# A transformer block on one Trainium2 core: roots by Newton steps on VectorE, first queries feature by feature, weights in 20 pieces, zero products by streamed share, single exponentials

## The chip, the cores and the metric

The kernel runs on one core of a Trainium2 chip. A core has five engines that run side by side, each through its own instruction queue in order: TensorE (PE in the profile; its weight loads are PEld), VectorE (DVE), ScalarE (ACT), GpSimd (POOL) and SyncE (SP), which here only issues DMAs. Sixteen DMA engines move data between the device's memory and the on-chip SBUF. TensorE writes its results to PSUM, eight banks of 128 partitions by 512 float32.

The metric is the device time of one execution in microseconds, the median of several runs.

## The reference

One pre-norm block over 2048 tokens of width 640, in bfloat16: attention with 32 query heads of 20 features that share one key and one value head, then a gated GELU layer with 1536 hidden features.

```python
def _layernorm(x, axis=-1, eps=1e-5):
    m = jnp.mean(x, axis=axis, keepdims=True)
    v = jnp.var(x, axis=axis, keepdims=True)
    return (x - m) / jnp.sqrt(v + eps)

def _A_ref(x, wq, wk, wv, wo):            # H = 32, Dh = 20
    q = (x @ wq).reshape(B, S, H, Dh) ... # heads first
    k = x @ wk                            # one head for all queries
    v = x @ wv
    scores = einsum("bhqd,bkd->bhqk", q, k) * Dh ** -0.5
    o = einsum("bhqk,bkd->bhqd", softmax(scores), v)
    return o ... .reshape(B, S, H * Dh) @ wo

def _B_ref(x, w_gate, w_up, w_down):
    return (gelu(x @ w_gate) * (x @ w_up)) @ w_down

h  = x + _A_ref(_layernorm(x), wq, wk, wv, wo)
h2 = h + _B_ref(_layernorm(h), w_gate, w_up, w_down)
```

There is no mask: 32 heads x 2048 queries x 2048 keys make 134 million exponentials.

## The kernel before, in words

**Tiling.** The tokens are 16 tiles of 128 rows. A *pack* is the work on four score tiles at once: eight matmuls of 20 features by 256 queries (L1009) fill four PSUM banks of 128 keys x 512. There are 512 packs, so 2048 score tiles. Each tile is exponentiated by one of two engines: ScalarE with its table (L1400, into `pa`), one tile per instruction or two that lie in neighbouring banks, or VectorE by arithmetic on the bits of the number (L1462, into `pd`), to which GpSimd adds two shifted copies by 64-bit integer adds (L1545). The sums over the keys (L1073, 128 x 32 by 256 columns) collect in an accumulator bank, with a column of ones for the denominator. Eight packs in a row make a *unit*; when a unit's products are all in, its accumulator is copied (L1108 or L1109 into `osb`), turned by a DMA transpose (`onu<-osb`, L681), divided by its denominator on VectorE (L720, L715 into `onq`), turned again (`onT<-onq`, L734) and multiplied by `wo`.

**LayerNorm.** For x (first) and for h (second): statistics on VectorE (L427, L434, L431), the root, a normalized copy `xn_tmp` (L541 on ScalarE or L543 on VectorE), and a DMA transpose `xn1T<-xn_tmp` (L525) that SyncE issues. The root of the first five groups of x tiles is a power on GpSimd (L464), which loads a library of instructions for it; a second library for the integer adds is loaded after the last of them (L460), and VectorE takes no score tile before that. All other groups take three Newton steps on VectorE (L471 to L492).

**Queries.** `xn1T` times `wq` gives queries token by token in PSUM; a copy to `qtok` (L642, L643) and a DMA transpose `qT<-qtok` (L655) bring the features onto partitions, where the packs need them.

**What sets the order.** A planner in the kernel file simulates five queues while the program is built: at each moment the engine that is free first takes the best task that its table of costs says is ready. The result is a fixed order of instructions on each engine, with semaphore waits between them; nothing is decided on the chip. The table `PRM` holds the planner's limits. `act_tile` takes one or two tiles, two only if at least `pair_min` are ready. `pe_decide` chooses between packs, sums over keys, pieces of projections (`issue_piece`) and *zero products*: matmuls of a zero tile into a free bank (L1280), issued where nothing else fits and TensorE was busy for less than `z_use` of the last 3400 ns by the planner's own times (`pe_use`).

**DMAs.** SyncE issues nearly all of them, in one queue. x tiles come first, then `wk`, `wv`, `wq` in two halves; the four large weights (`wo`, `wg`, `wu`, `wd`, one DMA each, L905) follow after 30 us of planned time. When the last score tile is done the rest of the gated layer for the last tokens runs alone (L560).

## Time and profile before

| | |
|---|---|
| median of 3 runs | 799.32 us (797.0 to 800.6) |
| profiled execution | 798.73 us, span of the trace 796.9 us |
| granted TensorE clock, mean | 0.949 |
| busy PE / DVE / ACT / POOL | 750.0 / 678.5 / 688.9 / 570.7 us |
| score tiles on ScalarE / VectorE | 1269 (939 alone, 165 pairs) / 779 |
| first and last start of a ScalarE exponential | 22.2 us, 750.4 us |
| HBM read / written | 12.18 / 2.62 MB |

The profile is one execution. An engine is busy when one of its instructions runs; waiting, branching and issuing DMAs do not count. In the page's second part the span is cut into 40 slices of 20 us and each digit is the busy share in tenths. "PEclk" is the clock granted to TensorE, 1.00 being full speed; it was either 1.00 or 0.50, so that an average between them is a share of time. In tables of stages each engine has its busy time and, in brackets, how many of its instructions ran there. In rows of waits "A <- B" means that A's engine stood still until B's instruction was done. In groups of instructions, "busy, mean ns" is the time covered by any of them, and the mean length of one; instructions of an engine overlap, so that one costs less than its length.

### The profile page before, as it was taken

To read this page: it belongs to the slowest core of one execution; us is meant where nothing else is said; L and a number is where in the kernel's file an instruction comes from. 1 tells how busy PE (TensorE), PEld (TensorE's weight loads), DVE (VectorE), ACT (ScalarE), POOL (GpSimd) and SP (SyncE) were. 2 spreads that over 40 slices of the span, in tenths; PEclk is the share of its full clock that TensorE was granted. 3 is DMA by queue.
4 is the path that set the end of the run, shared out by engine and by line. 5 is a ranking of instruction groups with operands and counts; after the bars stand their busy time and mean duration, and the time that the engine had idled before them with its cause. 6 is when DMAs were issued, how large, how long until landed. Compare 5 with 4: busy or idle time off the path is not lost.

```text
span 796.9 us, 37265 instructions
## 1 busy us (share of the span) xinstructions
PE 750.0 (94%) x16170; PEld 406.0 (51%) x16170; DVE 678.5 (85%) x1432; ACT 688.9 (86%) x1217; POOL 570.7 (72%) x1396
## 2 busy tenths in 40 slices
PE   7886999989998999999999999999999999999998
PEld 5343445444454545445554554444554545455687
DVE  6936899988989899999899887998899989989653
ACT  2685899987899899999999997999999999989822
POOL 1325899888888788588888786577888877588600
PEclk8688899978899899999999998999999999999999
DMA  7796101010021103010012302020022101101110
GB/s 200 117 245 200 30 9 32 9 25 9 10 40 22 20 11 53 10 26 10 22 31 60 53 13 41 9 27 9 10 43 52 38 10 26 26 11 25 50 28 18
DMA packets 79602, 33.44 MB, mean 42 GB/s; under 512 B 69072, under 2 KB 78160, under 8 KB 79440
## 3 DMA queue, kind: packets, MB, share of 16 engines
q1 hardware_dynamic: 79296, 30.90, 18.7%
q8 instruction: 128, 2.10, 1.1%
q14 instruction: 34, 0.28, 0.1%
q10 hardware_dynamic: 144, 0.16, 0.1%
HBM read 12.18 MB, written 2.62 MB: 19 GB/s over the span
## 4 chain that ended last, share of the span: by engine, by line
PE 52%; DVE 28%; ACT 11%; DMA 6%; issue 2%; SPq 1%; POOL 0%; DVEq 0%
DVE pd L1462 20%; PE ps L1073 18%; PE ps L1009 15%; PE ps L563 12%; ACT pa L1400 10%; PE ps L560 6%; DMA onu<-osb 2%; DMA onT<-onq 1%; DVE onq L715 1%; PE ps L1280 1%; DMA xn1T<-xn_tmp 1%; DVE stats L434 1%; DMA qT<-qtok 1%; DVE osb L1109 1%; DVE xh L757 1%
## 5 line engine op out<-in xcount | busy, mean ns | idle before, releaser
L1400 ACT ACTIVATE pa<-ps 128x512 bf16<-128x512 f32 (+1 forms) x1104 | 634.0, 715 | 51.6 <-PE ps L1009 43.8
L1545 POOL INT64_ADD pd<-pd x1378 | 566.1, 432 | 156.6 <-DVE pd L1462 133.1
L1462 DVE TENSOR_SCALAR pd<-ps 128x512 uint16<-128x512 f32 x779 | 497.8, 681 | 57.9 <-PE ps L1009 55.0
L1009 PE MATMUL ps<-qT,kT 20*128 20x256 bf16 x4096 | 263.8, 281 | 29.5 <-DVE pd L1462 13.1
L1073 PE MATMUL ps<-pd,v_ext 128*32 128x256 bf16 x4674 | 265.6, 286 | 0.6 <-DVE pd L1462 0.2
L1073 PE MATMUL ps<-pa,v_ext 128*32 128x256 bf16 x2538 | 227.3, 286 | 1.9 <-issue 0.8
L1073 PEld LDWEIGHTS ps<-pd,v_ext 128*32 128x32 bf16 x4674 | 168.7, 99 | 50.7 <-issue 28.6
L1009 PEld LDWEIGHTS ps<-qT,kT 20*128 20x128 bf16 x4096 | 88.5, 93 | 199.2 <-DVE pd L1462 96.9
L1073 PEld LDWEIGHTS ps<-pa,v_ext 128*32 128x32 bf16 x2538 | 127.2, 99 | 28.8 <-issue 18.9
L563 PE MATMUL ps<-wd_sb,gbuf 128*32 128x320 bf16 x1104 | 53.0, 302 | 0.3 <-DVE pd L1462 0.2
L563 PE MATMUL ps<-xn1T,wg_sb 128*32 128x512 bf16 x720 | 50.2, 382 | 0.1
L563 PE MATMUL ps<-xn1T,wu_sb 128*32 128x512 bf16 x720 | 49.0, 381 | 0.2
L862 DVE TENSOR_TENSOR gbuf<-ps,gbuf 128x512 bf16<-128x512 f32 (+2 forms) x72 | 36.5, 508 | 8.6 <-ACT gbuf L831 6.1
L831 ACT ACTIVATE gbuf<-ps 128x128 bf16<-128x128 f32 (+1 forms) x36 | 11.3, 313 | 27.0 <-PE ps L560 27.0
L563 PEld LDWEIGHTS ps<-wd_sb,gbuf 128*32 128x32 bf16 x1104 | 23.4, 95 | 18.8 <-issue 12.2
L563 PE MATMUL ps<-wo_sb,onT 128*32 128x320 bf16 x600 | 27.7, 301 | 1.7 <-DMA onT<-onq 1.5
L1280 PE MATMUL ps<-zero 128*32 128x256 bf16 x460 | 23.0, 334 | 4.1 <-POOL halfc L376 1.0
L563 PEld LDWEIGHTS ps<-xn1T,wu_sb 128*32 128x32 bf16 x720 | 16.4, 96 | 18.0 <-issue 6.3
L715 DVE TENSOR_TENSOR onq<-onu,rcp 128x160 bf16<-128x160 bf16 (+1 forms) x56 | 24.8, 470 | 0.2
L882 DVE TENSOR_TENSOR xh<-xh,ps 128x320 bf16<-128x320 bf16 x32 | 15.3, 479 | 11.1 <-PE ps L560 11.1
L1109 DVE CAST osb<-ps 128x256 bf16<-128x256 f32 x47 | 19.5, 414 | 6.0 <-PE ps L1073 5.9
L563 PEld LDWEIGHTS ps<-xn1T,wg_sb 128*32 128x32 bf16 x720 | 15.4, 95 | 16.9 <-issue 7.8
(65 smaller groups left out, 379.8 us busy)
## 6 DMA issues: line engine op xcount, KB each, us to landing
out_dram<-xh SPq DMA_DIRECT2D x16, 160.0 KB, 1.8
xh<-in_A_x_dram SPq DMA_DIRECT2D x7, 320.0 KB, 4.2
xh<-in_A_x_dram SPq DMA_DIRECT2D x13, 160.0 KB, 3.0
wg_sb<-in_B_w_gate_dram SPq DMA_DIRECT2D x1, 1920.0 KB, 9.3
wu_sb<-in_B_w_up_dram SPq DMA_DIRECT2D x1, 1920.0 KB, 11.1
wd_sb<-in_B_w_down_dram SPq DMA_DIRECT2D x1, 1920.0 KB, 16.0
wq_sb<-in_A_wq_dram SPq DMA_DIRECT2D x2, 400.0 KB, 5.8
wo_sb<-in_A_wo_dram SPq DMA_DIRECT2D x1, 800.0 KB, 5.2
```

The costliest lines, as they stand in the source:

```text
L560: return e.matmul(o(b), l(None), r, start=st, stop=sp)
L563: ins = e.matmul(o(b)[32 * q:32 * q + 32], l(q), r, start=st, stop=sp, tile_position=(0, 32 * q))
L715: dve((lambda o, vi, ri: lambda e: e.tensor_tensor(o, vi, ri.unsqueeze(3).to_broadcast([P, vi.shape[1], 4, Dh]), ALU.mult))(o, vi, ri), c_ ...
L862: dve(lambda e: e.tensor_tensor(o, bank(bk, n), o, ALU.mult), c_dve(n), [("b", bk)] + gkeys(b, fc), gkeys(b, fc), 0.8, fin)
L882: dve(lambda e: e.tensor_tensor(xh[:, t % NXH, h * HALF:(h + 1) * HALF], xh[:, t % NXH, h * HALF:(h + 1) * HALF], bank(bk, HALF), ALU.add) ...
L1009: ins = e.matmul(ps[:, b * 512 + h * 256:b * 512 + h * 256 + 256], kT4[32 * r:32 * r + Dh, kt * P:(kt + 1) * P], qv[32 * r:32 * r + Dh], s ...
L1073: ins = e.matmul(ps[32 * r:32 * r + 32, ab * 512:ab * 512 + 256], v_ext[:, it["kt"], it["w"], :], it["ap"], start=st, stop=(j in ends), ti ...
L1109: return e.tensor_copy(o, i)
L1280: ins = e.matmul(ps[32 * q:32 * q + 32, b * 512:b * 512 + 256], zero[:, 0:32], zero[:], start=True, stop=True, tile_position=(0, 32 * q))
L1400: op = plan.commit("act", lambda e: e.activation(dst, src, ACT.Exp, scale=SM_SCALE), cost, L_ACT, [("b", b0 + i) for i in range(n)], [("pa ...
L1462: op = plan.commit("dve", lambda e: e.tensor_scalar(pd[:, 0, s * 512:(s + 1) * 512], bank(b), CH_A, CH_B, ALU.mult, ALU.add), c_dve(512), ...
L1545: op = plan.commit("pool", (lambda w, a, sh: lambda e: e.int64_add(pd64[:, w, a], pd64[:, 0, a], sh))(w, a, sh), k * 128 * 1.7 + 180.0, L_ ...
```

## The change

1. **Roots.** The power on GpSimd is gone. All 18 groups of tiles take the same chain of ten small VectorE instructions (seed from the bits in 16 bits, two Newton steps, a reciprocal). The first LayerNorm's groups are now [0], [1], and seven pairs. Tile 0 is normalized on VectorE straight from mean and root. The only library of GpSimd is loaded at the start (L394); at the program's end four small GpSimd instructions with two more library loads are added.
2. **First queries.** The queries of tile 0 for heads 0 to 15 are computed feature by feature (`wq` stationary, `xn1T` streamed, 80 matmuls of 128 columns) and copied to `qT` without a transpose. `wq` comes in 340 + 300 columns.
3. **Weights.** `wo` in 2 pieces, `wg`, `wu`, `wd` in 6 each, spaced by 3.5 us of planned time; each use waits for its piece alone. The second part of `wq` and x tiles 6 to 9 are issued later (5.5, 8 and 9.5 us of planned time).
4. **Zero products.** `pe_use` counts the time that streaming the columns takes at full clock, not planned busy time, over 3413 ns; the limit is 0.53 (0.6 in the head), and below 0.48 zero products are issued where nothing else is ready, even if the next pack might have to wait for them. They may also be added to an open accumulator. 228 + 232 of them become 276 + 392.
5. **Single exponentials.** `pair_min` 9 cannot be reached with eight banks: all 1267 of ScalarE's tiles are single.
6. Other limits of the planner move (`w_tol`, `slack`, `press_a`, `press_d`, `q_ahead`, `flex_d`, `age`, `res_d`, `m_head`), and with them much of the order.

```diff
@@ PRM
-    "w_tol": 1300.0,
+    "w_tol": 600.0,
-    "slack": 60.0,
+    "slack": 20.0,
-    "press_a": 3,
-    "press_d": 3,
+    "press_a": 5,
+    "press_d": 2,
-    "q_ahead": 2,
+    "q_ahead": 4,
-    "flex_d": 400.0,
-    "pair_min": 4,
-    "age": 1500.0,
+    "flex_d": 800.0,
+    "pair_min": 9,
+    "age": 1000.0,
-    "ln1g": [[0], [1], [2, 3], [4, 5], [6, 7], [8, 9, 10, 11], [12, 13, 14, 15]],
+    "ln1g": [[0], [1], [2, 3], [4, 5], [6, 7], [8, 9], [10, 11], [12, 13], [14, 15]],
-    "z_use": 0.6,
+    "z_use": 0.53,
+    "w_t0": 30000.0,
+    "w_dt": 3500.0,
+    "z_head": 0.6,
+    "z_fk": 2,
+    "z_force": 0.48,
...
+    pool(lambda e: e.int64_add(lib[:, 1, :].bitcast(mybir.dt.int64), lib[:, 0, :].bitcast(mybir.dt.int64), 0),
+         7000, ["lib0"], ["lib1"])
...
+    def pe_use(t):
+        u = 0.0
+        for a, z, st in reversed(pe_log):
+            if z < t - 3413.0:
+                break
+            u += st * (z - max(a, t - 3413.0)) / (z - a)
+        return u / 3413.0
...
+        steps = [
+            (lambda e: e.tensor_copy(vb, mv[:, ln, sl, 1]), [("mv", ln, t) for t in tiles], [K("vb")]),
+            (lambda e: e.tensor_scalar_add(veb, vb, EPS), [K("vb")], [K("veb")]),
+            (lambda e: e.tensor_scalar(y0.bitcast(U16), veb.bitcast(U16), -0.5, 24352.0, ALU.mult, ALU.add),
+             [K("veb")], [K("y0")]),
...
+            (lambda e: e.scalar_tensor_tensor(den, tt, 1.5, p, ALU.add, ALU.mult), [K("t"), K("p")], [K("den")]),
+            (lambda e: e.reciprocal(ln_r[:, ln, sl], den), [K("den")], [K("lr")]),
+        ]
...
-            task(("pool",), lambda e: e.tensor_tensor(ln_denb[:, ln, sl], ln_veb[:, ln, sl], halfc[:, 0:n], ALU.pow),
-                 700, L_POOL, [("veb", kk), "halfc"], [("den", kk)], prio - 1.0, pdone)
...
+    def q0_job(h):
+        g0 = 0 if h == "a" else 2
...
+                pieces.append((mm((lambda i: lambda b: ps[:, b * 512 + i * P:b * 512 + i * P + P])(i),
+                                  (lambda i, c: lambda q: wq_sb[:, c * D + 80 * (g0 + i) + 20 * q:
+                                                                c * D + 80 * (g0 + i) + 20 * q + 32])(i, c),
+                                  xn1T[:, c, 0:P], c == 0, c == NC_D - 1, False), c_mm(P) + 20.0,
+                               [("xn1T", 0), ("wq", 0)]))
...
-    for nm, o, v in (("wo", wo_sb, A_wo), ("wg", wg_sb, B_w_gate), ("wu", wu_sb, B_w_up), ("wd", wd_sb, B_w_down)):
-        sp_tasks.append(_Task(("sp",), (lambda o, v: lambda e: e.dma_start(o[:], cview(v)))(o, v), 1500, 12000,
-                              [], [nm], 9.0, None, lambda: plan.free["sp"] > 30000.0))
...
+    for i, (o, v, ks) in enumerate(pieces_w):
+        sp_tasks.append(_Task(("sp",), (lambda o, v: lambda e: e.dma_start(o, v))(o, v), 480, 3500,
+                              [], ks, 9.0 + 0.01 * i, None,
+                              (lambda i: lambda: plan.free["sp"] > PRM["w_t0"] + i * PRM["w_dt"])(i)))
...
+        if state["qk_left"] > 0 and not head and pe_use(t) < PRM["z_force"] and not (nr or piece is not None or opening is not None):
+            if zeros(PRM["z_fk"]):
+                return True
```

On **SyncE**, where the large weights are issued (the last x tiles' transposes, then weights, then the first finished unit), before:

```order
L525 DMA_TRANSPOSE xn1T<-xn_tmp 128x5x128 x4
L655 DMA_TRANSPOSE qT<-qtok 128x4x128
L905 DMA wo_sb<-in_A_wo_dram 128x5x640
L905 DMA wg_sb<-in_B_w_gate_dram 128x5x1536
L914 DMA xh<-in_A_x_dram 128x640 x3
L655 DMA_TRANSPOSE qT<-qtok 128x4x128
L914 DMA xh<-in_A_x_dram 128x640 x3
L905 DMA wu_sb<-in_B_w_up_dram 128x5x1536
L905 DMA wd_sb<-in_B_w_down_dram 128x12x640
L681 DMA_TRANSPOSE onu<-osb 128x4x128 x2
```

and now:

```order
L537 DMA_TRANSPOSE xn1T<-xn_tmp 128x5x128 x10
L669 DMA_TRANSPOSE qT<-qtok 128x4x128 x2
L955 DMA wo_sb<-in_A_wo_dram 128x2x640
L955 DMA wo_sb<-in_A_wo_dram 128x3x640
L669 DMA_TRANSPOSE qT<-qtok 128x4x128
L537 DMA_TRANSPOSE xn1T<-xn_tmp 128x5x128 x2
L955 DMA wg_sb<-in_B_w_gate_dram 128x5x256 x2
L971 DMA xh<-in_A_x_dram 128x640 x6
L669 DMA_TRANSPOSE qT<-qtok 128x4x128
L955 DMA wg_sb<-in_B_w_gate_dram 128x5x256 x3
L717 DMA_TRANSPOSE onu<-osb 128x4x128
```

A finished unit's transpose stands behind pieces, no longer behind whole weights. Up to the last of the sixteen `xn1T` there are now four `qT` and both pieces of `wo` in the queue, where there were six `qT`.

On **TensorE**, where one accumulator is finished and the next has too few products to open, so that packs (`ps<-qT,kT`) follow one another with hardly a sum over keys (`v_ext`) between them; before, around packs 107 to 110:

```order
L1009 MATMUL ps<-qT,kT 128x256 x8
L1073 MATMUL ps<-pd,v_ext 32x256 x4
L1009 MATMUL ps<-qT,kT 128x256 x16
L1280 MATMUL ps<-zero 32x256 x8
L1009 MATMUL ps<-qT,kT 128x256 x8
L1280 MATMUL ps<-zero 32x256 x12
```

and now, around packs 99 to 102:

```order
L1066 MATMUL ps<-qT,kT 128x256 x8
L1130 MATMUL ps<-pd,v_ext 32x256
L1066 MATMUL ps<-qT,kT 128x256 x8
L1270 MATMUL ps<-zero 32x256 x12
L1066 MATMUL ps<-qT,kT 128x256 x8
L1270 MATMUL ps<-zero 32x256 x24
L1066 MATMUL ps<-qT,kT 128x256 x8
L1270 MATMUL ps<-zero 32x256 x8
```

This place has 44 zero products now, the one before had 20.

On **VectorE** at the start, from the variance of tile 0 on (`ln_vb`), before:

```order
L449 CAST ln_vb<-mv 128x1
L431 BN_AGGR mv<-stats 128x2
L453 TENSOR_SCALAR ln_veb<-ln_vb 128x1
L449 CAST ln_vb<-mv 128x1
L434 BN_STATS stats<-xh 128x6
L453 TENSOR_SCALAR ln_veb<-ln_vb 128x1
```

and now:

```order
L488 CAST ln_vb<-mv 128x1
L463 BN_STATS stats<-xh 128x6
L489 TENSOR_SCALAR ln_veb<-ln_vb 128x1
L460 BN_AGGR mv<-stats 128x2
L463 BN_STATS stats<-xh 128x6
L490 TENSOR_SCALAR ln_y<-ln_veb 128x1
```

Each BN_STATS shown belongs to tile 2 or 3, whose load it needs. Now the chain of tile 0 stands behind it; the copy `xn_tmp` of tile 0 comes 28 instructions later than the first BN_STATS shown, and four of these are statistics.

More of the change, by code (lines that the diff above doesn't have):

```diff
@@ L491, in nden @@
-        def nden(op):
-            dve(lambda e: e.tensor_tensor(ln_denb[:, ln, sl], va, ya, ALU.mult), 65, [("nv", kk), ("ny", kk)],
-                [("den", kk)], prio - 1.0, c4)
-        def c4(op):
-            dve(lambda e: e.reciprocal(ln_r[:, ln, sl], ln_denb[:, ln, sl]), 75, [("den", kk)], [("lr", kk)],
-                prio - 1.0, c5)
+                chain(steps, c5)(None)
         def c5(op):
-            if ln == 0:
+            if ln == 0 and tiles[0] not in DIRECT:
                 dve(lambda e: e.scalar_tensor_tensor(ln_nb[:, sl], mv[:, ln, sl, 0], -1.0, ln_r[:, ln, sl], ALU.mult,
@@ L959, in dve_ok @@
     def dve_ok():
[L960 removed]
+        return pd_free[pd_next[0]]
     def est_banks(t):
@@ L1027, in issue_qk @@
             last = i == len(parts) - 1
[L1028 to L1029 removed]
+            op = pe(mk(part), (219.0 if last else 115.0) + sw, 53.3 * len(part), t_reads,
+                    [("b", b) for r, b in part], t, L_PE + (0.0 if last else 104.0))
             for r, b in part:
@@ L1201, in pe_decide, with zeros, zfn @@
                 piece = None
+        def zeros(k):
+            fb = [b for b in free_now if plan.ready("pe", ["zero"], [("b", b)]) <= t]
+            ac = [u["acc"] for u in accu if all(u["started"])]
+            if not (fb or ac):
+                return False
+            b = fb[-1] if fb else ac[0]
+            fresh = bool(fb)
+            def zfn(e):
+                ins = None
+                for q in list(range(4)) * k:
+                    ins = e.matmul(ps[32 * q:32 * q + 32, b * 512:b * 512 + 256], zero[:, 0:32], zero[:],
+                                   start=fresh, stop=fresh, tile_position=(0, 32 * q))
+                return ins
+            state["z"] = 1
+            sw = 0.0 if state["mode"] == "v" else SW
+            state["mode"] = "v"
+            pe(zfn, 110.0 * k + sw, 106.7 * k, ["zero"], [("b", b)], t)
+            return True
+        if state["qk_left"] > 0 and not head and pe_use(t) < PRM["z_force"] and not (nr or piece is not None or opening is not None):
+            if zeros(PRM["z_fk"]):
+                return True
         wready = nr >= 1 or opening is not None or piece is not None
@@ L1270, in pe_decide @@
             return do_pv()
[L1271 to L1294 removed]
+        if (state["qk_left"] > 0 or PRM["z_tail"]) and fits(110.0 + swv - slack) and pe_use(t) < (PRM["z_head"] if head else PRM["z_use"]):
+            return zeros(1)
+        return False
     def next_piece(t, may, pick_bank):
@@ L1503, in dve_decide @@
                 opts.append((pr, len(opts), tk))
+            elif tk.prio < 0.0 and state["kv_left"] > PRM["chain_k"] and plan.ready("dve", tk.reads, tk.writes) <= t + PRM["chain"]:
+                opts.append((tk.prio, len(opts), tk))
         opts.sort(key=lambda o: o[:2])
```

195 lines of the change are left out of this document (105 added, 90 removed).

## The prediction, made before the changed kernel had run

> **What bounds the kernel now.** I read the page's busy times first, then a table of stages, then the waits and the chain inside the stages that fall short, and last groups and single rows for prices.
>
> ```profile
> PE 750.0 (94%) x16170; PEld 406.0 (51%) x16170; DVE 678.5 (85%) x1432; ACT 688.9 (86%) x1217; POOL 570.7 (72%) x1396
> core 0: us, PE busy (x) PEld busy (x) DVE busy (x) ACT busy (x) POOL busy (x), PEclk, DMA share, GB/s
> 20.00:60.00 40.00, 33.81 (x592) 17.34 (x594) 26.57 (x104) 30.24 (x54) 13.45 (x35) 0.74 0.83 182
> 60.00:100.00 40.00, 32.61 (x658) 16.16 (x652) 29.25 (x51) 29.46 (x49) 28.30 (x59) 0.83 0.38 113
> 100.00:148.90 48.90, 46.77 (x1076) 24.73 (x1074) 48.13 (x88) 47.20 (x84) 47.29 (x101) 1.00 0.09 17
> 148.90:203.50 54.60, 49.89 (x920) 24.58 (x924) 46.17 (x97) 43.83 (x71) 44.59 (x98) 0.78 0.11 16
> 203.50:254.70 51.20, 46.41 (x1112) 24.76 (x1104) 48.70 (x100) 49.65 (x89) 44.77 (x106) 1.00 0.18 25
> 254.70:264.90 10.20, 9.26 (x156) 4.07 (x160) 9.36 (x20) 7.55 (x12) 8.65 (x22) 0.67 0.25 48
> 100.00:740.00 640.00, 614.63 (x13888) 319.58 (x13886) 580.35 (x1148) 600.54 (x1046) 515.77 (x1264) 0.97 0.14 25
> 750.40:797.00 46.60, 43.62 (x508) 37.21 (x508) 21.59 (x69) 13.19 (x39) 0.00 (x0) 1.00 0.11 29
> ```
>
> The work that must be done is nearly all on two engines, ScalarE and VectorE, which share the score tiles. Between 100 and 148.9 us they are busy for 95.3 of 97.8 engine-us: that stage is full, and only less work on them could shorten it. So I count lost time as idle time of these two together, against this full stage (2.5 idle of 97.8, 2.6%), and halve it, since an idle us of both is worth one us of the span.
>
> By that count 20 to 60 us lose (80 - 56.8 - 2.1) / 2 = 10.6 us, 60 to 100 us lose (80 - 58.7 - 2.1) / 2 = 9.6 us, 148.9 to 203.5 us lose (109.2 - 90.0 - 2.8) / 2 = 8.2 us, 254.7 to 264.9 us (20.4 - 16.9 - 0.5) / 2 = 1.5 us; 203.5 to 254.7 us lose only 0.7 us. From 750 us on TensorE works alone, through the last tokens' projections. The change leaves their matmuls as they are (five `wd` products are whole instead of in four quarters), so those 46.6 us stay. The gain can come from four places and no other.
>
> **The stop at 69 us, and the weights in pieces.**
>
> ```profile
> wg_sb<-in_B_w_gate_dram SPq DMA_DIRECT2D x1, 1920.0 KB, 9.3
> 63.20 10.60 DMA onu<-osb
> DVE rcp L720 <- DMA onu<-osb: 6.6, 1, 6.6
> 68.90:73.80 4.90, 0.16 (x6) 0.00 (x0) 0.00 (x0) 0.74 (x2) 0.00 (x0) 1.00 0.55 102
> 73.80:87.40 13.60, 11.86 (x170) 5.07 (x174) 9.95 (x18) 7.88 (x13) 8.74 (x16) 0.50 0.01 3
> ```
>
> The first finished unit's transpose is issued at 63.20 us behind `wu` and `wd` and lands 10.6 us later. VectorE's next instruction is the reciprocal of it; queued behind that are its score tiles, so banks stay full, TensorE stops, ScalarE gets no tile: 4.9 us with all engines still. The stop costs a second time: afterwards TensorE's clock is 0.50 for 13.6 us, in which ScalarE and VectorE are busy for 17.8 of 27.2. In the new order that transpose has one piece in flight ahead of it. `wg` gives 1920 KB in 9.3 us, a piece of 320 KB then some 1.6 us, and no such stop is left. At most the whole 9.6 us of 60 to 100 us come back, at least the 4.9 us of the stop; I take 8.5, nearer the full sum, because the slow clock behind it has the stop as its cause. What is late next is the transposes behind pieces, by up to 1.6 us each; SyncE's own issue slots for 16 more DMAs at about 0.5 us lie in its idle time.
>
> **The start: roots, library and first queries.**
>
> ```profile
> 6.42 0.49 DVE stats L434
> 8.90 1.12 POOL L464 TENSOR_TENSOR ln_denb<-ln_veb,halfc 128x1 bf16<-128x1 bf16 x2 [7.24 <-issue]
> 11.12 2.73 DMA xn1T<-xn_tmp
> 39.04 5.24 SPq L525 DMA_TRANSPOSE xn1T<-xn_tmp  x4
> 27.34 0.18 POOL L460 INT64_ADD lib<-lib  x1 [6.02 <-issue]
> 18.69 0.40 DVE stats L427
> 19.09 0.11 DVE mv L431
> L543 DVE TENSOR_SCALAR xn_tmp<-xh,mv,ln_r 128x640 bf16<-128x640 bf16 x24 | 10.7, 463 | 0.1
> 28.69 0.15 DVE L492 TENSOR_TENSOR ln_denb<-nwt 128x4 bf16<-128x4 f32 x1
> 28.76 0.15 DVE L474 TENSOR_SCALAR nwt<-nwt 128x4 int32<-128x4 int32 x1
> ```
>
> The first root waits until 8.90 us for GpSimd's library (7.24 us of "issue"), and the first transpose starts at 11.12 us. Now the root stays on VectorE, but tile 0's chain stands behind statistics of tiles 2 and 3, whose load lands at 6.42 us. From there: four statistics at 0.40 us of the chain, three aggregations at 0.11, 21 small steps at 0.08 (one starts at 28.69, the next at 28.76), the normalized copy 0.46: 6.42 + 1.60 + 0.33 + 1.68 + 0.46 = 10.5 us. That is 0.6 us earlier. The second library load (6.0 us) vanishes from the stretch in which VectorE was kept from score tiles. Four of SyncE's transposes take 5.24 us, so it issues one per 1.3 us; with four `qT` instead of six ahead of the last x transpose, two `wo` pieces at about 0.8 us in their place, and the earlier start, the keys are complete about 0.6 + 2 x 1.3 - 1.6 = 1.6 us sooner by this queue alone; the clock in this stretch (0.74, with 48 more zero products before the first real matmul) and the missing wait for the first `qT` add something. Between 1.6 us and the whole 10.6 us that 20 to 60 us lose I take 4, nearer the queue's sum, since the queue of transposes is still the pace. The chain of ten steps adds 46 small steps to VectorE here (4 us), in a stretch where it idles for 13 of 40. The two library loads at the end, 13.3 us by these rows, run on GpSimd under the 46.6 us in which it does nothing; uncovered they would cost all of it.
>
> **The clock, and zero products by streamed share.**
>
> ```profile
> 145.49:148.91 3.42, 3.35 (x88) 1.00 0.00 0
> 148.91:152.32 3.41, 2.46 (x48) 0.99 0.32 46
> 152.32:155.73 3.41, 3.41 (x60) 0.50 0.00 0
> 155.73:159.15 3.42, 3.13 (x84) 1.00 0.02 5
> 159.15:162.56 3.41, 2.09 (x40) 0.99 0.00 0
> 162.56:165.97 3.41, 2.91 (x48) 0.50 0.04 8
> 203.52:206.93 3.41, 2.91 (x80) 1.00 0.00 0
> 206.93:210.35 3.42, 2.72 (x64) 1.00 0.02 5
> L1280 PE MATMUL ps<-zero 128*32 128x256 bf16 x460 | 23.0, 334 | 4.1 <-POOL halfc L376 1.0 <-DVE pd L1462 1.0 <-ACT pa L1400 0.9
> ```
>
> Here is TensorE in windows of 3.41 us, the steps in which its clock changes. A window with 40 or 48 matmuls is followed by a window at half clock; one with 64 is not. Half clock makes the next packs late, the sums pile up, the following window is dense, then dry again: five rounds of this make the 8.2 us. The dry windows are the places where one accumulator ends and the next cannot open. The new rule counts streamed columns and puts 32 to 44 zero products there instead of 12 to 20: with the 24 or so matmuls of packs in such a window that is 56 to 68, about at the 64 that held. At best the 9.7 us of the two stretches come back, at worst nothing; I take 7, nearer the best, since most of the new counts reach 60. The zero products after the start rise from 232 to 392; at 23.0 us for 460 the 160 more cost up to 8.0 us if TensorE had no gap for them, nothing if each fills one. They are issued where nothing else is ready: I take 1 us.
>
> The Trainium skill (TensorE: Matmul & The Clock Gate, Part 1: The HAM clock gate) has the clock fall after an idle window of about 3.4 us. Here TensorE is busy for 2.46 of 3.41 us in a window that is followed by half clock, so the row says that a thinly used window is enough.
>
> **Single exponentials.**
>
> ```profile
> 350.86 15.79 ACT L1400 ACTIVATE pa<-ps 128x512 bf16<-128x512 f32 x32
> 193.70 2.85 ACT L1400 ACTIVATE pa<-ps 128x1024 bf16<-128x1024 f32 x3
> L1400 ACT ACTIVATE pa<-ps 128x512 bf16<-128x512 f32 x939 | 488.8, 656 | 26.6 <-PE ps L1009 22.1 <-PE ps L1073 1.5
> L1400 ACT ACTIVATE pa<-ps 128x1024 bf16<-128x1024 f32 x165 | 172.5, 1052 | 25.0 <-PE ps L1009 21.7
> ```
>
> Back to back, a single follows a single every (15.79 - 0.66) / 31 = 0.49 us and a pair a pair every (2.85 - 1.05) / 2 = 0.90 us. Two singles instead of a pair cost 0.08 us more, 165 times: 13 us of ScalarE, and the planner gives VectorE only two tiles more. Against it stands the idle time: 25.0 us before 165 pairs (0.15 each) and 26.6 before 939 singles (0.03 each), since a pair waits for its second bank. If singles keep their 0.03, 330 of them idle for 9 us, which saves 16. Bounds: 13 us lost (ScalarE decides everywhere) and 3 us won; I take 2 lost, nearer the gain: where ScalarE is full the loss is real, but the idle rows show that most pairs did not come in a full stretch. Seven fewer query copies on ScalarE (and six more on VectorE) change nothing in sum.
>
> The Trainium skill (ScalarE: Activation LUTs, What ACT_TABLE_LOAD costs) gives 186 ns fixed per instruction and an overlap of 93 between neighbours, so about 93 for each instruction more and, as an estimate, 15 us for 165. The trace's 0.08 us is close to it; the rule speaks against this part of the change and the sum by it would be 2 us longer at ScalarE's bound.
>
> **Roots of the second LayerNorm.** Nine groups need 10 steps where they had 15: 45 steps at 0.08 us are 3.6 us of VectorE in full stages. Bounds 0 and 3.6 us; halved, since ScalarE must be relieved as well, and rounded down: 1 us won.
>
> **Sum.** -8.5 (stop) - 4 (start) - 7 (clock) + 1 (zero products) + 2 (singles) - 1 (roots) = -17.5 us. The profiled execution took 798.73 us (span 796.9), 0.6 below the median of the runs: 798.73 - 17.5 = **781 us**.
>
> **Rivals.**
>
> *The clock is not held* (20%). The counts at the dry places are 56 to 68 by the planner's times, and a real gap of 0.3 us more takes 8 matmuls from a window. Then five rounds remain: 781 + 7 = 788 us. The row that held at x64 and the ones that fell at x48 leave the point between them open, which speaks for this rival. By the Trainium skill's idle window (page and section above) zero products in windows as busy as these buy nothing, which ends at the same 788 us; the half clock after x48 speaks against that.
>
> *ScalarE becomes the bound* (12%). It is busy for 600.5 of 640 us between 100 and 740 us; with the stalls gone it is full, and the 13 us of singles all count: 781 + 11 = 792 us. For it speaks the full stage at 100 us, against it the 16 us of idle time that pairs brought.
>
> *The gain is given back later* (8%). The order is fixed; if in the head an in-order wait (VectorE for a transpose, as at 69 us) only moves to the first unit behind `wo`, and the clock drops there, then the stop (8.5) and the clock (7) both stay: 797 us, no change.
>
> *Slower: pieces collide with transposes* (6%).
>
> ```profile
> qT<-qtok SPq DMA_TRANSPOSE x32, 3.0
> ```
>
> Twenty pieces share the DMA engines with the transposes between about 35 and 110 us. Each delays the transpose behind it by its own 1.6 us, and VectorE or ScalarE stands at its first use in order, as at 69 us. Eighteen such delays of 320 KB are 29 us. With 1 us of slack or more each they vanish; without any the stretch turns from 8.5 won to 8.5 lost when more than ten of them count, and 781 + 17 + 8 = 806 us if all do. Against it: a query's transpose lands 3.0 us after its issue in the median, the head's load stretch included, and most are used several packs later.
>
> **How the numbers follow.** 54% for the forecast (its own range 772 to 786), 20, 12, 8 and 6% for the rivals. The bounds summed would be 759 (all gains) and 813 (all losses); the range of 767 to 796 us takes in the first two rivals and half of the third. A change under 0.5% (4 us) cannot be told from none in a few runs of this kernel. Faster: the forecast and the first two rivals, 86%; no change 8%; slower 6%.
>
> **What would show it.** Right: no stretch with idle engines near 69 us, `onu<-osb` landing in about 3 us everywhere; a mean clock of 0.97 or more and few halves between 140 and 270 us; the first `xn1T` transpose near 10.5 us; ScalarE's exponentials at 0.49 us apart with less idle time before them than 51.6 us; the end of the exponentials near 733 us and 46 us of tail. Wrong: half clock again after dry windows with 56 or more matmuls, ScalarE at 97% or more between 100 and 720 us with no gain, or VectorE waiting for `onu` or `qT` while pieces land.

## The result, and the profile after

The changed kernel takes 764.61 us (median of 4 runs, 764.14 to 771.65), the kernel before beside it 799.96 us: a ratio of 0.958 with a 95% interval of 0.952 to 0.965. The forecast was 781 us with a range of 767 to 796, so the gain is 35 us where 17.5 were expected, and the time lies outside the range.

The page after: the span, the busy times, and the granted clock in slices of 19 us.

```profile
span 762.8 us, 38203 instructions
PE 731.9 (96%) x16542; PEld 405.0 (53%) x16542; DVE 675.6 (89%) x1429; ACT 692.6 (91%) x1387; POOL 567.9 (74%) x1398
PEclk9789899999999999999999999999999999999999
```

The table of stages after. The last two rows are the stretch from 270 us to the start of ScalarE's last score tile, and everything up to it.

```profile
core 0: us, PE busy (x) PEld busy (x) DVE busy (x) ACT busy (x) POOL busy (x), PEclk, DMA share, GB/s
20.00:60.00 40.00, 35.33 (x745) 19.36 (x743) 28.80 (x103) 35.30 (x86) 17.26 (x42) 0.79 0.86 164
60.00:100.00 40.00, 38.35 (x851) 20.25 (x846) 36.85 (x65) 36.69 (x73) 35.73 (x77) 0.91 0.50 117
100.00:148.90 48.90, 47.53 (x1107) 25.74 (x1102) 48.54 (x94) 48.26 (x99) 45.67 (x100) 1.00 0.17 33
148.90:203.50 54.60, 51.70 (x1277) 28.71 (x1276) 53.97 (x103) 53.23 (x107) 51.79 (x108) 1.00 0.13 24
203.50:254.70 51.20, 48.90 (x1128) 25.05 (x1116) 49.21 (x99) 49.89 (x102) 44.62 (x116) 0.97 0.12 24
254.70:264.90 10.20, 10.07 (x228) 4.75 (x220) 9.86 (x19) 10.20 (x22) 8.55 (x24) 1.00 0.08 16
270.00:715.50 445.50, 436.40 (x10235) 229.91 (x10234) 406.95 (x788) 435.12 (x846) 357.51 (x910) 1.00 0.15 28
0.00:715.50 715.50, 687.50 (x16038) 367.51 (x16041) 654.41 (x1364) 679.38 (x1349) 567.16 (x1394) 0.98 0.23 45
```

The same two last rows of the kernel before, where ScalarE's last score tile starts at 750.4 us.

```profile
270.00:750.40 480.40, 467.61 (x10762) 244.31 (x10762) 432.77 (x855) 457.32 (x805) 376.89 (x955) 0.99 0.14 27
0.00:750.40 750.40, 706.37 (x15666) 368.81 (x15670) 656.95 (x1363) 675.68 (x1179) 570.68 (x1396) 0.95 0.21 43
```

VectorE and ScalarE together work 1333.8 us up to the last tile after, 1332.6 us before. Their work did not shrink, so the gain is their idle time. Half of it by stage, as the prediction counted (without its allowance for a full stage):

| stage, us | before | after | gain |
|---|---|---|---|
| 20 to 60 | 11.6 | 8.0 | 3.6 |
| 60 to 100 | 10.6 | 3.2 | 7.4 |
| 100 to 148.9 | 1.2 | 0.5 | 0.7 |
| 148.9 to 203.5 | 9.6 | 1.0 | 8.6 |
| 203.5 to 264.9 | 3.7 | 1.9 | 1.8 |
| 270 to the last tile | 35.4 | 24.5 | 10.9 |

For example, after 270 us it is (2 x 445.5 - 406.95 - 435.12) / 2 = 24.5. Together that is 33 us. The tail behind the last tile is about as long as before (762.8 - 715.5 = 47.3 us for 46.5). The changed kernel is ahead in tiles from 60 us on, so the same times do not hold the same tiles in both; the table says where time was lost, not which tile lost it.

The groups of score exponentials after, then the DMA issues of the pieces, and then what VectorE waits for finished units.

```profile
L1459 ACT ACTIVATE pa<-ps 128x512 bf16<-128x512 f32 x1267 | 637.9, 671 | 20.1 <-PE ps L1066 14.1
L1521 DVE TENSOR_SCALAR pd<-ps 128x512 uint16<-128x512 f32 x781 | 497.2, 681 | 36.4 <-PE ps L1066 31.2
```

```profile
wg_sb<-in_B_w_gate_dram SPq DMA_DIRECT2D x6, 320.0 KB, 4.3
wu_sb<-in_B_w_up_dram SPq DMA_DIRECT2D x6, 320.0 KB, 5.0
```

```profile
DVE rcp L756 <- DMA onu<-osb: 1.0, 3, 0.6
```

ScalarE's idle time before exponentials fell from 51.6 to 20.1 us, VectorE's from 57.9 (in the same view before) to 36.4. The stop at 69 us is gone: VectorE waits 0.6 us at most for an `onu` (6.6 before), and the slowest lands 4.4 us after its issue (10.6 before; the median was 2.5 already then). A piece takes 4.2 to 5.0 us, not the 1.6 that were worked out from the whole weight.

### The profile page after: what moved, and what is told of

Its sections match the earlier page's. It is cut to its first block, busy times and chain, and to the rows that moved or that the text cites. A ratio compares the mean times of both kernels' runs of the same rounds, so it can differ in the third digit from the quotient of the medians.

```text
span 762.8 us, 38203 instructions
## 1 busy us (share of the span) xinstructions
PE 731.9 (96%) x16542; PEld 405.0 (53%) x16542; DVE 675.6 (89%) x1429; ACT 692.6 (91%) x1387; POOL 567.9 (74%) x1398
## 4 chain that ended last, share of the span: by engine, by line
PE 56%; DVE 30%; ACT 8%; DMA 5%; issue 1%; SPq 0%
DVE pd L1521 20%; PE ps L1130 17%; PE ps L1066 17%; PE ps L576 15%; PE ps L573 6%; ACT pa L1459 6%; DVE onq L751 2%; DMA onT<-onq 2%; ACT gbuf L883 1%; DMA xn1T<-xn_tmp 1%; PE ps L1270 1%; DVE stats L463 1%; DVE stats L456 1%; DMA onu<-osb 1%; DVE osb L1166 1%
## 5 line engine op out<-in xcount | busy, mean ns | idle before, releaser
L1459 ACT ACTIVATE pa<-ps 128x512 bf16<-128x512 f32 x1267 | 637.9, 671 | 20.1 <-PE ps L1066 14.1
L1521 DVE TENSOR_SCALAR pd<-ps 128x512 uint16<-128x512 f32 x781 | 497.2, 681 | 36.4 <-PE ps L1066 31.2
L1066 PE MATMUL ps<-qT,kT 20*128 20x256 bf16 x4096 | 255.9, 275 | 12.9 <-DVE pd L1521 3.1
L1130 PE MATMUL ps<-pd,v_ext 128*32 128x256 bf16 x4686 | 256.5, 277 | 1.1 <-issue 0.8
L1130 PE MATMUL ps<-pa,v_ext 128*32 128x256 bf16 x2534 | 210.7, 277 | 0.7 <-DVE pd L1521 0.3
L1130 PEld LDWEIGHTS ps<-pd,v_ext 128*32 128x32 bf16 x4686 | 164.1, 97 | 43.4 <-issue 28.3
L1130 PEld LDWEIGHTS ps<-pa,v_ext 128*32 128x32 bf16 x2534 | 117.7, 97 | 27.4 <-issue 18.1
L576 PE MATMUL ps<-xn1T,wg_sb 128*32 128x512 bf16 x720 | 52.0, 382 | 0.1
L898 DVE TENSOR_TENSOR gbuf<-ps,gbuf 128x512 bf16<-128x512 f32 (+2 forms) x72 | 36.4, 509 | 16.0 <-PE ps L576 7.2
L576 PEld LDWEIGHTS ps<-wd_sb,gbuf 128*32 128x32 bf16 x1084 | 23.4, 96 | 17.6 <-issue 10.6
L576 PE MATMUL ps<-wo_sb,onT 128*32 128x320 bf16 x600 | 29.1, 307 | 1.9 <-DMA onT<-onq 1.8
L1270 PE MATMUL ps<-zero 128*32 128x256 bf16 x668 | 27.6, 295 | 2.9 <-issue 1.4
L918 DVE TENSOR_TENSOR xh<-xh,ps 128x320 bf16<-128x320 bf16 x32 | 15.4, 481 | 12.0 <-PE ps L573 11.1
L576 PE MATMUL ps<-wq_sb,xn1T 128*32 128x320 bf16 x540 | 25.5, 302 | 0.0
```

The source lines that it names most:

```text
L576: ins = e.matmul(o(b)[32 * q:32 * q + 32], l(q), r, start=st, stop=sp, tile_position=(0, 32 * q))
L898: dve(lambda e: e.tensor_tensor(o, bank(bk, n), o, ALU.mult), c_dve(n), [("b", bk)] + gkeys(b, fc), gkeys(b, fc), 0.8, fin)
L918: dve(lambda e: e.tensor_tensor(xh[:, t % NXH, h * HALF:(h + 1) * HALF], xh[:, t % NXH, h * HALF:(h + 1) * HALF], bank(bk, HALF), ALU.add) ...
L1066: ins = e.matmul(ps[:, b * 512 + h * 256:b * 512 + h * 256 + 256], kT4[32 * r:32 * r + Dh, kt * P:(kt + 1) * P], qv[32 * r:32 * r + Dh], s ...
L1130: ins = e.matmul(ps[32 * r:32 * r + 32, ab * 512:ab * 512 + 256], v_ext[:, it["kt"], it["w"], :], it["ap"], start=st, stop=(j in ends), ti ...
L1270: ins = e.matmul(ps[32 * q:32 * q + 32, b * 512:b * 512 + 256], zero[:, 0:32], zero[:], start=fresh, stop=fresh, tile_position=(0, 32 * q))
```

## Experiments

Two directions: one part of the change put into the kernel before, and one part undone in the changed kernel. Each is compared with the kernel before on the same chip. One hundredth of a ratio is 8 us. The diffs are shortened. Most edits make the planner find another order for all engines, so that what such a run shows is the part together with its new order.

### The new rule for zero products

In the kernel before:

```diff
-    "z_use": 0.6,
+    "z_use": 0.53, "z_head": 0.6, "z_fk": 2, "z_force": 0.48,
+            u += st * (z - max(a, t - 3413.0)) / (z - a)     # pe_use: streamed, not busy time
+            if ... pe_use(t) < PRM["z_force"]: zeros(PRM["z_fk"])
```

> The kernel before with the new rule for zero products only (streamed share, limit 0.53, forced below 0.48). Forecast's terms: 7 won, 1 lost, 794 us, clock 0.97, no rounds of half clock between 149 and 203 us. Rival 'the zero rule won the extra gain': 785 us or less. Rival 'the clock is not held': 799 to 802 us with the clock still at 0.95.

Measured 785.5 us, ratio 0.987 (0.983 to 0.990). And undone in the changed kernel (busy time again, limit 0.6, nothing forced, free banks only):

> The changed kernel with the old rule for zero products (planned busy time, limit 0.6, none forced, free banks only). Forecast's terms: 6 us lost, 769 to 772 us, half clock again where accumulators change. Rival 'the zero rule won the extra gain': 778 us or more.

Measured 784.31 us, ratio 0.986 (0.980 to 0.991). So the rule alone brings 11 us and is worth 22 us among the rest (0.986 for 0.958): it is the largest part. Two stages of the kernel before with only this rule:

```profile
60.00:100.00 40.00, 34.13 (x729) 17.28 (x728) 32.64 (x59) 32.03 (x57) 31.70 (x67) 0.91 0.37 107
148.90:203.50 54.60, 51.75 (x1224) 28.00 (x1212) 53.94 (x111) 51.55 (x87) 50.53 (x113) 1.00 0.09 14
```

In the second 1.9 us of half idle time where there were 9.6, and no half clock: the five rounds are gone. In the first 7.7 for 10.6. In the changed kernel the last zero product starts at 237.5 us, and with the old rule back the half idle time after 270 us is 26.8 us for 24.5: the rule does its work before.

What decides is seen in single steps of the clock, in the changed kernel:

```profile
86.07:89.49 3.42, 2.57 (x48) 1.11 (x42) 3.42 (x7) 3.32 (x8) 3.38 (x9) 1.00 1.31 180
89.49:92.90 3.41, 3.15 (x48) 1.07 (x52) 1.99 (x4) 1.90 (x4) 2.22 (x5) 0.51 0.98 335
147.53:150.94 3.41, 2.73 (x58) 1.17 (x56) 3.41 (x10) 3.41 (x9) 3.41 (x10) 1.00 0.02 5
226.03:229.44 3.41, 2.87 (x60) 1.03 (x56) 3.41 (x11) 3.37 (x8) 2.98 (x9) 1.00 0.23 46
229.44:232.85 3.41, 3.41 (x64) 1.75 (x64) 3.37 (x8) 2.51 (x6) 2.94 (x7) 0.50 0.00 0
```

A step with 48 matmuls is followed by half clock, as before; one with 58 is not (the step from 150.94 us on ran at 1.00), one with 60 is. So neither the count nor the busy time (2.73 us held, 2.87 fell) is quite the measure. As an estimate, with the kernel's own 26.7 ns for a matmul of 256 columns whose rows or columns take a quarter of the array, spread evenly over its record, the 58 stream for 0.44 of the step and the 60 for 0.41. Counted so over the 18 profiled executions of this study, the clock fell 136 times from 20 us on, always after a step with a streamed share under 0.44, 117 times under 0.40; of 3,613 steps that kept full clock only 16 were under 0.40 and none under 0.33. From 0.33 to 0.43 both occur. By the Trainium skill's idle window (TensorE: Matmul & The Clock Gate, Part 1: The HAM clock gate) the clock falls after an idle window; the ratio of 0.987 from filling windows that were thin but not idle speaks against that as the only condition.

More of the same does not help:

```diff
-    "z_use": 0.53, "z_force": 0.48,
+    "z_use": 0.58, "z_force": 0.53,
```

> The changed kernel with more zero products: the limit at 0.58 in place of 0.53, the forced ones below 0.53 in place of 0.48. Theory: the clock still falls at 89 and 229 us, where the planner saw 0.48 to 0.53; with them filled the clock is 0.985 to 0.99 and 2 to 4 us are gained, ratio 0.952 to 0.956. Rival: the new order loses elsewhere what the clock gains, ratio 0.96 to 0.97, as with the old limits, whose clock was 0.991.

Measured 765.19 us, ratio 0.960 (0.956 to 0.964), clock 0.987 for 0.98: no difference from the changed kernel that can be told. This does not show that the half clocks that are left cost nothing: the order is another one, and its half idle time from 270 us to the last tile is 30.6 us for 24.5, as the rival in the expectation has it.

### The weights in pieces

The kernel before with the 20 pieces and nothing else:

```diff
-    for nm, o, v in (("wo", ...), ("wg", ...), ("wu", ...), ("wd", ...)):   # one DMA each
+    for i, (o, v, ks) in enumerate(pieces_w):                               # 20 DMAs, 3.5 us apart
```

> The kernel before with the four large weights in 20 pieces and nothing else; every engine but SyncE keeps its order. Forecast's term: the stop at 69 us goes, with the slow clock behind it, 8.5 us won, 791 to 792 us, transposes of finished units landing in about 3 us. If the extra gain of the whole change (35 us against 17.5) lies in the pieces, 780 us or less. If pieces collide with transposes, 800 us or more.

Measured 797.28 us, ratio 0.998 (0.995 to 1.001): nothing. The table of stages tells why:

```profile
60.00:100.00 40.00, 37.07 (x745) 18.72 (x740) 33.96 (x59) 34.20 (x59) 33.74 (x70) 0.84 0.48 114
100.00:148.90 48.90, 46.41 (x972) 23.34 (x968) 44.04 (x81) 42.51 (x74) 42.49 (x91) 0.89 0.14 33
203.50:254.70 51.20, 47.14 (x1004) 23.62 (x996) 44.33 (x91) 45.63 (x81) 41.83 (x100) 0.87 0.19 25
```

From 60 to 100 us the half idle time falls from 10.6 to 5.9 us, so the stop does go. But from 100 to 148.9 us, which was full, it rises from 1.2 to 5.6 us at a clock of 0.89, and from 203.5 to 254.7 us from 2.0 to 6.2 at 0.87. That is the rival *the gain is given back later*, in this kernel. It is not a matter of a new order: in the traces every engine but SyncE has the order of before, so that the same tile can be followed. Counted by the starts of the score tiles, the 101st comes 8.5 us sooner than before, the 301st 2.0 us sooner and the 601st 0.6 us later. The same order, run earlier, meets half clock in other places.

If so, the pieces must show once the clock is held:

> The kernel before with the new rule for zero products and the weights in 20 pieces. Alone, the zero rule gave a ratio of 0.9865 and the pieces 0.998. Theory: the pieces do remove the stop at 69 us, but alone the gain is given back by half clock in the dry windows between 100 and 260 us; with the clock held the stop's 8 us show: ratio 0.975 to 0.979 (about 778 us), and no stretch near 69 us in which all engines stand. Rival: the pieces are worth nothing here and what they save in the changed kernel hangs on its other start: ratio 0.985.

Measured 782.86 us, ratio 0.982 (0.977 to 0.987), between the two expectations; the intervals of this and of the zero rule alone overlap. These two have the same order on every engine but SyncE, and in the profiled executions the 7.7 us by which the 101st tile comes sooner with the pieces are still 6.5 us at the last tile (the one with pieces is the fastest of its four). So with the clock held the lead is kept there; by the medians it is 3 us. Whole weights in the changed kernel:

> The changed kernel with the four large weights as whole DMAs after 30 us of planned time. Forecast's term: 8.5 us lost, 772 to 774 us, the first finished unit's transpose landing some 10 us after its issue and all engines still for 5 us. If the pieces' place in the new order hides it, 765 us.

Measured 772.71 us, ratio 0.970 (0.966 to 0.975): 10 us are lost by going back, but not by the expected stop: the slowest `onu` lands 6.6 us after its issue, VectorE waits 2.6 us for it at most, and from 60 to 100 us the half idle time is 4.7 us for 3.2. The planner also makes another order here. So the pieces are worth nothing without the zero rule, 3 to 7 us with it at the same order, and 10 in the whole, together with the order.

### Single exponentials

Alone in the kernel before (`pair_min` 4 to 9), and undone in the changed kernel (`pair_min` 4, `press_a` 3):

> The kernel before with single exponentials only (pair_min 9), the planner's order made anew. Forecast's term: 2 us lost, 800 to 804 us. Rival 'singles won the extra gain' (a bank comes free after one tile, so ScalarE and TensorE wait less): 788 us or less, with the idle time before exponentials falling from 51 us to about 20. Rival 'ScalarE is the bound': 808 to 813 us.

> The changed kernel with pairs again (pair_min 4; press_a is back at 3, since the planner finds no order with 5 and pairs), 148 pairs. Forecast's term: 2 us won by undoing, 761 to 765 us. Rival 'singles won the extra gain': 775 us or more, with ScalarE idle before pairs for 0.15 us each.

Measured 791.85 us, ratio 0.993 (0.991 to 0.996), and 774.24 us, ratio 0.972 (0.967 to 0.976): singles win 5 us alone and 11 among the rest, where the forecast had a loss of 2. The changed kernel with pairs again, its groups and its stretch to the last tile:

```profile
L1459 ACT ACTIVATE pa<-ps 128x512 bf16<-128x512 f32 x986 | 513.1, 644 | 18.0 <-PE ps L1066 11.8 <-PE ps L1130 2.2
L1459 ACT ACTIVATE pa<-ps 128x1024 bf16<-128x1024 f32 x148 | 155.7, 1056 | 15.9 <-PE ps L1066 12.8
L1521 DVE TENSOR_SCALAR pd<-ps 128x512 uint16<-128x512 f32 x766 | 488.1, 680 | 49.4 <-PE ps L1066 45.1
```

```profile
270.00:729.20 459.20, 445.16 (x10430) 236.80 (x10418) 407.42 (x783) 439.32 (x773) 351.81 (x890) 0.99 0.14 28
```

Its half idle time after 270 us is 35.8 us, that of the kernel before (35.4) and not of the changed one (24.5). VectorE idles more before its own tiles too (49.4 us for 36.4), though it has no pairs. `press_a` differs too in this run. Alone, singles leave 31.4 us after 270 us, and the limits alone, with pairs, leave 30.1; so it is not singles by themselves that make the 24.5.

Three runs keep the order of every engine as it was and change only how a pair is carried out. First, two instructions that together wait for both banks and free both:

```diff
-  e.activation(dst, src, Exp)                          # 1024 columns
+  for i in range(2): e.activation(dst[i], src[i], Exp) # 512 each; waits and releases as the pair
```

> The kernel before with its order of work unchanged; only each of the 165 pair exponentials is given to ScalarE as two instructions of 512 columns, which together wait for and release both banks as the pair did. This is the disputed cost of one more instruction by itself. The prediction's price (0.08 us each, 13 us of ScalarE) would make it 3 to 13 us slower. The traces so far have singles starting 0.477 us after each other and a single 0.904 to 0.921 us after a pair, so 0.03 to 0.05 us each and 5 to 8 us of ScalarE; halved between two engines and with idle time to lie in, 2 to 5 us slower, ratio 1.003 to 1.006. Rival: a pair's instruction is itself slow over a bank's border, and two singles cost nothing: ratio 1.000 or below.

Measured 801.53 us, ratio 1.007 (1.004 to 1.009). ScalarE works 684.4 us up to the last tile for 675.7, so an instruction more costs (684.42 - 675.68) / 165 = 0.053 us:

```profile
0.00:753.90 753.90, 707.47 (x15666) 369.87 (x15670) 657.96 (x1363) 684.42 (x1345) 571.07 (x1396) 0.95 0.21 43
```

Then each of the two waits for its own bank and frees it alone, and after that the first waits for both and each frees its own:

> The kernel before with the order of every engine unchanged; each of the 165 pairs is two instructions of 512 columns, and each of the two waits for its own bank alone and frees it alone. Against the run in which two instructions waited and freed together (ratio 1.0066), only this differs. Theory: what makes singles pay is that a bank is waited for and freed by itself, in any order: ratio 0.993 to 0.998. Rival: the order that the planner makes with singles is what gained, and in the old order the early bank finds nobody waiting: ratio 1.004 to 1.007.

> The same, but the first of the two also waits for both banks; each still frees its own bank alone. Theory one, the gain of the run before comes from the earlier release (TensorE gets a bank 0.48 us sooner): the same ratio as with waits of their own. Theory two, it comes from not waiting for the second bank (25.0 us of idle time before 165 pairs): ratio as with two that wait and free together, 1.004 to 1.007.

Measured 797.69 us, ratio 1.000 (0.997 to 1.002), and 798.36 us, ratio 1.000 (0.998 to 1.003). At the same order, the same instructions are 0.7% (5 us) faster if each frees its own bank, whether the first waits for the second bank or not. So the release is what counts, not the wait: an instruction that is done by itself gives its bank to the next pack, and also its `pa` to the sums over keys, half a pair sooner. Which of the two counts was not tried apart. TensorE's waits for ScalarE ahead of packs and of sums, two instructions that free together:

```profile
PEld ps L1009 <- ACT pa L1403: 16.9, 59, 1.0
PEld ps L1073 <- ACT pa L1403: 3.2, 9, 0.6
```

and the ones that wait and free singly (L1401 a tile or the first half, L1408 the second half):

```profile
PEld ps L1009 <- ACT pa L1401: 8.6, 34, 0.4
PEld ps L1009 <- ACT pa L1408: 2.4, 9, 0.4
PEld ps L1073 <- ACT pa L1401: 6.9, 18, 0.9
PEld ps L1073 <- ACT pa L1408: 1.2, 4, 0.4
```

Ahead of packs that is 5.9 us less, but ahead of sums 4.9 us more, so these rows do not add up to the 5 us. Cost and release cancel: at a fixed order singles are neutral. The remaining 5 us of singles alone and the 11 us in the changed kernel come with the order that the planner makes from single tiles. That order isn't always better:

> The same with single exponentials as well. Theory: a single frees its bank half an instruction sooner and waits for one bank and not two, so it brings 5 to 6 us more on top of a held clock: ratio 0.967 to 0.971 (about 772 us). Rival: singles alone gained only because their steadier flow kept the clock up (0.970 for 0.95), which the zero products already do: ratio as with the zero rule and pieces, 0.975 to 0.979. The prediction's own sign (2 us lost) would give 0.978 to 0.981.

Measured 793.1 us, ratio 0.995 (0.992 to 0.998): 10 us slower than the same without singles. Zero rule, pieces and singles:

```profile
52.00:56.00 4.00, 2.18 (x38) 1.09 (x38) 0.42 (x1) 1.22 (x3) 0.00 (x0) 0.63 0.76 159
60.00:100.00 40.00, 38.62 (x894) 20.93 (x883) 29.85 (x53) 38.96 (x82) 28.09 (x63) 1.00 0.47 117
100.00:700.00 600.00, 573.18 (x13361) 300.34 (x13364) 551.37 (x1086) 572.38 (x1116) 487.74 (x1188) 0.99 0.15 27
```

Zero rule and pieces alone:

```profile
60.00:100.00 40.00, 38.05 (x861) 20.11 (x859) 36.92 (x67) 37.05 (x66) 36.52 (x77) 0.96 0.54 124
100.00:700.00 600.00, 579.16 (x13357) 303.48 (x13356) 550.61 (x1086) 571.62 (x995) 488.39 (x1199) 0.99 0.16 27
```

From 100 to 700 us the two idle alike: 76.3 and 77.8 us of both engines together. Half idle time from 20 to 100 us is 19.3 us for 12.0, and both engines nearly stand from 52 to 56 us (0.42 and 1.22 us of 4): most of the loss is in the head. SyncE's rows of the slower one:

```profile
46.05 0.58 SPq L936 DMA_DIRECT2D wo_sb<-in_A_wo_dram  x1
46.67 0.49 SPq L936 DMA_DIRECT2D wg_sb<-in_B_w_gate_dram  x1
47.20 6.56 SPq L545 DMA_TRANSPOSE xn1T<-xn_tmp  x4
```

Here the last x transposes are issued behind two pieces and take 6.56 us for four (5.24 in the kernel before). That is where the rival *pieces collide with transposes* would sit. Whether the pieces or the late copies of x made the stop was not tried.

### The other limits, the start and the library

The limits of the planner alone in the kernel before, and set back in the changed kernel (there with `stag_n0`, another limit of the start):

> The kernel before with the planner's other limits only (w_tol, slack, press_a, press_d, q_ahead, flex_d, age, res_d, m_head). The forecast gave them no price: 798 to 802 us. Rival 'the limits won the extra gain' (fewer stalls of ScalarE and VectorE in the stages of the gated layer): 788 us or less, with less idle time after 250 us.

> The changed kernel with the planner's other limits as before (singles, pieces, zero rule, roots and first queries stay new). The forecast gave them no price: 763 to 767 us. Rival 'the limits won the extra gain': 775 us or more, idle time of ScalarE and VectorE higher after 250 us.

Measured 794.59 us, ratio 0.999 (0.996 to 1.001), and 769.34 us, ratio 0.966 (0.962 to 0.970): nothing alone, 6 us among the rest. The latter has a clock of 0.991 and is slower all the same, so the clock is not all.

What is left when pairs, old zero rule, whole weights and old limits are put back is the roots, the library and the first queries:

> The changed kernel with pairs, the old rule for zero products, whole weights and the old limits: what is left of the change is the roots on VectorE, one library, the first queries feature by feature and the later first loads. The prediction has 4 us for the start and 1 us for the second roots: ratio 0.994 (about 791 us). Rival one: the start alone is worth nothing, because the clock takes it back in the stretch from 100 to 260 us as it did with the pieces: ratio 1.000. Rival two: the start is where the unforeseen gain lies, 10 us or more: ratio 0.987.

Measured 793.05 us, ratio 0.995 (0.991 to 0.998): 4 us, where the forecast had 5 for the start and the second roots together. But not where it was forecast:

```profile
20.00:60.00 40.00, 31.61 (x594) 17.04 (x591) 25.14 (x96) 30.55 (x67) 14.59 (x34) 0.82 0.81 181
60.00:100.00 40.00, 37.23 (x718) 18.23 (x714) 32.80 (x57) 32.99 (x54) 31.59 (x66) 0.79 0.43 114
```

From 20 to 60 us the half idle time is 12.2 (11.6 before). From 60 to 100 us it is 3.5 us less than before, but from 100 to 148.9 us 4.7 us more (5.9 for 1.2, at a clock of 0.90), as rival one has it. The 351st score tile starts 1.7 us later than before, the 1291st 2.4 us sooner and the 1331st 7.2 us sooner. So the 4 us at the end are not shown to come from the start.

Last, the changed kernel without GpSimd's four instructions and two library loads at its end:

```diff
-    pool(int64_add ...); pool(...)    # the four at the program's end
```

> The changed kernel without the four instructions of GpSimd at the program's end, which load two libraries; the output is untouched. Theory: the library that GpSimd has at the end of one execution is there at the start of the next, so this changes nothing at the start (the integer adds' library is the last one used in both): first integer add still at 1.8 us with a gap under 0.3 us, time as with the change, 762 to 768 us. Rival: the loads at the end are what makes the start free, and without them the first integer add waits 6 to 7 us; that lies before the first tile of GpSimd, so that the time stays the same.

One run, 764.87 us. GpSimd's first integer add, in both kernels the same row, and the waits for the two loads of the changed kernel:

```profile
1.77 0.19 POOL L394 INT64_ADD lib<-lib  x1
POOL lib L1653 <- issue: 6.6, 1, 6.6
POOL lib L1651 <- issue: 5.9, 1, 5.9
```

The start is free with and without the loads at the end, and these, 6.6 and 5.9 us, lie under the tail; no cost of them shows.

## Why the prediction was right or wrong

**The method held.** Half the idle time of ScalarE and VectorE gives 33 of the 35 us, with equal work. What was wrong is which idle time was priced. The sum by stages: 20 to 100 us, forecast 12.5, measured 11.0; 100 to 265 us, forecast 6, measured 11.1; after 265 us, forecast a loss of 1, measured a gain of 10.9.

**The step that failed: "The gain can come from four places and no other".** The prediction took its lost time from four short stretches; the long one after 265 us got no price but the singles' loss and the second roots. Its own table speaks against that. By its own count the row from 100 to 740 us loses (1280 - 1180.9 - 33.3) / 2 = 32.9 us, and only 10.4 of these lie before 265 us: some 22 us were left without a price. Part of them is a visible stop. Of the kernel before:

```profile
450.00:500.00 50.00, 48.19 (x1060) 24.34 (x1056) 39.83 (x73) 41.92 (x75) 34.68 (x90) 0.93 0.22 30
477.00:490.00 13.00, 11.42 (x201) 5.03 (x196) 7.46 (x16) 8.26 (x16) 6.16 (x16) 0.75 0.41 64
```

The first row has 9.1 us of half idle time, the second 5.1 of them. Copies of queries wait there for the transposes of earlier ones (2.75 us on ScalarE, 1.43 on VectorE), and half clock follows from 485 us on. The changed kernel, which is 26 us ahead there, has 3.1 us of half idle time from 425 to 470 us, at full clock. The same 450 to 500 us have 2.9 us with the limits alone, 2.6 with the start alone and 4.2 with singles alone: new orders lose less there, with pairs too. The rest is spread thinly. The largest row of idle time of the whole run, which the prediction left out, stands ahead of VectorE's tiles, and nearly all of it is put down to TensorE:

```profile
L1462 DVE TENSOR_SCALAR pd<-ps 128x512 uint16<-128x512 f32 x779 | 497.8, 681 | 57.9 <-PE ps L1009 55.0
```

37.7 of these 57.9 us lie after 270 us; in the changed kernel it is 24.9 of 36.4. Which part of the change wins the 10.9 us stays open. With pairs they are gone (35.8 us again), and with whole weights, the old zero rule or the old limits the stretch has 29.1, 26.8 and 26.4 us. But the run with more zero products keeps every part and has 30.6 at the same total time, so that a difference of 6 us here can come with the order alone.

**Single exponentials: wrong in sign.** The price of an instruction more was 0.08 us and is 0.053, so 8.7 us of ScalarE and not 13. (The Trainium skill, ScalarE: Activation LUTs, What ACT_TABLE_LOAD costs, would have 0.093 us and, as an estimate, 15 us; the trace is lower.) The reason given for a gain, that a pair waits for its second bank, falls: with that wait kept the time is the same. The earlier release pays for the instructions; the prediction did not ask who waits for what a pair holds. The rest is the order, which was known only once the planner had made it. The rival *ScalarE becomes the bound* fell too: with 679.4 us of work in 715.5 it still idles.

**The clock: right in mechanism, too small.** Five rounds of half clock vanish, and the two stretches that the 7 us were forecast for give 8.6 and 1.6 us. But the rule alone gives 11 us where 7 less 1 were taken. It also acts in the head (10.6 to 7.7 us from 60 to 100 us by itself), which the prediction left to the stop. The cost of 1 us for zero products can't be seen: with the rule alone there are 744 of them for 460, and TensorE is busy for 741.1 us and not 750.0. That 56 to 68 matmuls would be about enough came out at the edge only: of the steps shown, 58 held and 60 did not.

**The stop: right in place, its size in part luck.** 7.4 us from 60 to 100 us for 8.5 forecast. With the pieces alone the 101st tile does come 8.5 us sooner, but the lead is lost again by the 601st (ratio 0.998); it is kept where the clock is held. And the 7.4 us are not the pieces' alone: the zero rule by itself wins 2.9 us there, and with whole weights the changed kernel still has 5.9 of them. The piece's 1.6 us was wrong by a factor of three: a sixth of a weight took half as long as the whole. Why was not tried, and no long wait for an `onu` came of it.

**The start: the size is luck, the working is not borne out.** 3.6 us for 4 between 20 and 60 us. But the load for which all waits lands later, and the last of SyncE's x transposes are not sooner. Rows of VectorE and SyncE in the changed kernel:

```profile
7.02 0.49 DVE L463 BATCH_NORM_STATS2 stats<-xh 128x6 f32<-128x320 bf16 x1 [1.68 <-DMA xh<-in_A_x_dram]
```

```profile
10.73 1.31 SPq L537 DMA_TRANSPOSE xn1T<-xn_tmp  x1
42.05 3.05 SPq L537 DMA_TRANSPOSE xn1T<-xn_tmp  x2
```

Statistics at 7.02 us for 6.42, the first transpose at 10.73 us for the 10.5 forecast, and the last two issued by 45.1 us for 44.3 before. Run by itself, the start won nothing from 20 to 60 us.

**Roots of the second LayerNorm** (1 us) were not tried alone; VectorE's work up to the last tile fell by 2.5 us in all.

**The limits** had no price: nothing alone, 6 us in the whole. Undone one at a time, the four parts cost 10, 11, 22 and 6 us, 49 together; alone they bring 1, 5, 11 and 1, 18 together, and 22 with the start's 4. The gain of 35 lies between. That the parts help each other is seen for the pieces and the zero rule, at one order; for the rest the order differs from run to run, and how far the time scatters between orders with the same parts was not measured. The prediction added its terms as if each stood alone. That its 17.5 us are not far from these 22 is luck: the stop was put too high by 7 us, the zero rule too low by 5 and the singles by 7.

## What to carry to other kernels

Where a planner fixes the order in advance, a part comes with the order that it brings about, and one run does not tell the two apart; runs that keep the order do. Even at one order a stop that goes away in one place can return as half clock in the next hundred us, and here the lead was kept only with the clock held. Count idle time of the binding engines over the whole run, the long stretch as well as the short ones, and go through it in slices: here one of 50 us held 9 of its 35 us. Before a larger instruction is taken for cheaper, look at who waits for what it holds: here the 0.053 us that a pair saves are paid back by banks and results that come free half an instruction later.

## What was not expected of the hardware

The clock falls after thin windows, not only idle ones: in the executions of this study always after a step of 3.41 us with a streamed share under 0.44 (an estimate from the records), and of 133 steps under 0.40 only 16 kept it. GpSimd's first integer add starts at 1.77 us without a load, while the kernel before, whose first library is that of the power, waited 7.24 us. This fits a library that outlives an execution, but it is not shown: every kernel here ends with the library of the integer adds, so that this one could as well be there from the start. And the same 330 tiles of 512 columns cost or save 5 us by nothing but the moment at which their banks and results are released.
